# Regrouping the zero stores of a decode-attention backward kernel: four stores per step, counted over batch and kv-head together

## The chip, the core and the metric

The kernel runs on one NeuronCore of a Trainium2 chip. The metric is device time in microseconds (us). The median of the 11 runs of the kernel before is 290.94 us (289.98 to 292.38).

## What is computed

The reference is a decode step (B = 4 rows, one token each, D = 512) with its gradients. The layer is a layernorm, attention over a cache of 4096 positions of which only the last 1024 are attended, a gated feed-forward block beside it, and the residual:

```python
W = min(4096, max(256, Sk // 4))               # 1024 of Sk = 4096
k = jnp.repeat(k_cache[:, :, Sk - W:, :], rep, axis=1)
v = jnp.repeat(v_cache[:, :, Sk - W:, :], rep, axis=1)
p = softmax(einsum(q, k) * Dh ** -0.5);  o = einsum(p, v)
return x + o.reshape(B, Sq, Hq * Dh) @ wo + (gelu(xn @ w_gate) * (xn @ w_up)) @ w_down
```

The outputs are the forward result and the gradients of x, of both caches and of all weights. The gradient of a cache has the cache's shape, (4, 8, 4096, 128) in bf16. Its last 1024 positions hold dK or dV. The first 3072 positions were never attended, so their gradient is zero, and the kernel has to write these zeros: 2 caches x 4 batch rows x 8 kv-heads = 64 regions of 3072 x 128 x 2 bytes = 768 KB each, 50.3 MB in all.

## The kernel before, in words

**Stages.** Inputs are loaded, the feed-forward block is done (to about 47 us), and then a loop over t = 0..3 treats two kv-heads (g = 0, 1) of all four batch rows at a time. An iteration t does, in the order of the program: `scores(t, 0)` (transposes of the K blocks and S = qK), `softmax(t)`, `scores(t, 1)` (the same on the V blocks, dP), `softmax_d(t)`, `odq(t, 0)` (the output o), `pre(t + 1)` (projections for the next iteration from wo and wq), `odq(t, 1)` (dq), `fin(t)`, `load_next(t)`, which issues all loads of iteration t + 2. The products for dV, dK, dwo and dwq are put as small pieces in a list `bg`, and `tick(2)` takes two of them after each K or V block. Each piece is a matmul into PSUM and a copy to a staging tile by `evac` (L94 on ACT, L96 on DVE); full staging tiles (`stg_dv`, `stg_dk`, `osb_o`, `osb_q`) are stored from POOL.

**Three issuers of DMA.** SP issues all loads (wo L235, wq L237, K and V blocks `kb`, `vb` L242) and the two small last stores. POOL issues the stores of computed gradients. ACT issues the stores of zeros (L100, called from `zeros`), from a tile `ztile` of zeros on 64 partitions, in rows of 12 KB.

**Where zeros are issued.** `zeros(n)` stores the next n regions. It walks a queue of runs, and one DMA stays within one run and has at most 4 regions (GP * 2). Before the change a run is the 8 regions of one cache and one batch row. The calls: 4 regions at the end of the feed-forward part; in `scores(t, k)` at b == 1 of each g, 4 regions, but none for g = 0, k = 0 (there 2 in t = 3); 2 after `scores(0, 0)`; 2 after `odq(t, 0)` in t = 2 and t = 3; all that is left at the end. That is 18 regions up to the end of t = 0, then 12, 14 and 16 in t = 1, 2 and 3, and 4 at the end. The calls for 2 shift the runs against the calls for 4, so that several calls for 4 reach the end of a run and become two DMAs of 2 regions: 8 DMAs of 4 regions and 16 of 2. Each store is also placed behind the last `evac` on ACT.

**Completion semaphores.** The framework gives each DMA that SP or ACT issues one of eight completion semaphores in turn, in the order of the scheduled program, counted over both engines together. A DMA waits, on the engine that issues it, until the DMA that had its semaphore before it has landed. So the DMA at place n of the list waits for place n - 8, whatever the two have to do with each other, and what stands behind it on its engine waits too. POOL's stores have eight semaphores of their own. The later part of the list in the program before (x r: regions; "S" SP, "A" ACT), with the start of each issue in the profiled execution:

```
18 A zeros x4 (t0) 58.43    19 A zeros x2 61.64    20 A zeros x4 69.73    21, 22 A zeros x2, x2 76.19, 76.84
23 S wo(2) 94.95    24 S wq(2) 98.28    25, 26 S kb(2,0), kb(2,1) 103.83    27 A zeros x4 (t1) 107.27
28, 29 S vb(2,0), vb(2,1) 105.00, 117.73    30, 31 A zeros x2, x2 118.76, 119.41    32 A zeros x4 126.13
33 S wo(3) 144.14    34 S wq(3) 152.72    35, 36 S kb(3,0), kb(3,1) 153.31, 158.11
37 A zeros x2 (t2) 162.82    38, 39 S vb(3,0), vb(3,1) 158.52, 183.7
40 A zeros x2 163.47    41 A zeros x4 172.10    42, 43 A zeros x2, x2 186.27, 197.20    44 A zeros x2 200.18
45 A zeros x2 (t3) 219.17    46, 47 A zeros x2, x2 225.33, 225.98    48 A zeros x4 236.94
49, 50 A zeros x2, x2 243.76, 244.41    51 A zeros x2 246.84    52 A zeros x4 (end) 271.40
53 S out_0 273.96    54 S out_1 277.44
```

wo(t), wq(t), kb(t,g) and vb(t,g) are the loads of iteration t. Places 0 to 17 are the inputs of the feed-forward part, the loads of t = 0 and t = 1, and, at place 11, the first store of 4 regions of zeros.

Of the kernel before, what the change touches and what calls it, by code (L numbers as in the profile page):

```python
# [18 lines left out]
def kernel(  # L19
# [26 lines left out]
    nc = tc.nc  # L46

    B, Sq, D = A_x.shape
    _, G, Sk, Dh = A_k_cache.shape
# [4 lines left out]
    K0 = Sk - W  # L54
# [4 lines left out]
    GP = 2  # L59
    NT = G // GP  # L60
# [37 lines left out]
    def store(eng, out, in_, kind, apart):  # L98

        d = eng.dma_start(out=out, in_=in_)  # L100
        for k in apart:
            tc.declare_no_dep(d.ins, group=k, reason="stores write disjoint parts of the outputs")
        tc.add_to_no_dep_group(kind, d.ins)
        return d
# [54 lines left out]
    ZP = P // 2  # L159
# [92 lines left out]
                    load_kv(t + 2, k, g)  # L252


    zruns = deque([og, b, 0] for b in range(B) for og in (out_2, out_3))

    def zeros(n):


        zs = ztile[0:P:P // ZP, :]  # L260
        while n > 0 and zruns:
            og, b, g = zruns[0]
            w = min(n, G - g, GP * 2)
            zsrc = bass.AP(tensor=zs.tensor, offset=zs.offset, ap=[list(zs.ap[0]), [0, w], [1, ZW]])
            z = store(nc.scalar, og[b, g:g + w, 0:K0, :].rearrange("g (m j) d -> m g (j d)", m=ZP), zsrc, "zeros",
                      ["rest", "zeros"])
            tc.add_manual_dep(z.ins, last[-1].ins.name,
                              mybir.DependencyInfo(mybir.DependencyClass.NoSync, mybir.DependencyReason.DATA))
            n -= w
            zruns[0][2] += w  # L270
            if zruns[0][2] == G:
                zruns.popleft()


# [2 lines left out]
    def tick(n):  # L277
        for _ in range(min(n, len(bg))):
            bg.popleft()()
# [62 lines left out]
    def scores(t, k):  # L342

        lf = (qm, dom)[k][:].rearrange("p s c -> p (s c)")
        blks = (k_t, v_t)[k]
        ps = ps_a.tile([P, WQ], FP32, name="S_ps", tag=("S", "dP")[k])
        for g in range(GP):
            for b in range(B):
                T_ps = ps_w.tile([P, J, P], BF16, name="T_ps", tag="w")
                for j in range(J):  # L350
                    nc.tensor.transpose(T_ps[:, j, :], blks[(t, g)][:, b, j, :], ident[:])  # L351
                T_sb = tsb.tile([P, J * P], BF16, name="T_sb", tag="T", bufs=4)
                evac(T_sb[:], T_ps[:].rearrange("p j m -> p (j m)"), 1024, half=True)
                s = b * GP + g
                for q in range(NQ):
                    nc.tensor.matmul(ps[q * RG:(q + 1) * RG, :], lhsT=lf[:, s * RG:(s + 1) * RG],  # L356
                                     rhs=T_sb[:, q * WQ:(q + 1) * WQ], start=(g == 0 and b == 0),
                                     stop=(g == GP - 1 and b == B - 1), tile_position=(0, q * RG))
                tick(2)
                if b == 1:  # L360
                    zeros(4 if (g, k) != (0, 0) else 2 if t == NT - 1 else 0)
        st[t][("S", "dP")[k]] = ps[:]

    def by_quarter(src, nm):
# [293 lines left out]
    for f4 in range(NF4):  # L658
        held = {}
        n = min(4, NF - 4 * f4)  # L660
# [30 lines left out]
    with tc.tile_pool(name="stage", bufs=3, reuse_waits="tile") as stage, \  # L691
            tc.tile_pool(name="wodd", bufs=1, reuse_waits="tile") as wodd:
        wpool.append(wodd)
        kvpool.append(wodd)
        load_w(1)
        for k in range(2):
            load_kv(1, k, 1)
        for t in range(NT):
            if t == 0:
                pre(t)  # L700
            masks(t)
            scores(t, 0)
            zeros(2 if t == 0 else 0)
            softmax(t)
            dvdk(t, 0)
            scores(t, 1)
            softmax_d(t)
            dvdk(t, 1)
            odq(t, 0)
            zeros(2 if t >= NT - 2 else 0)  # L710
            if t + 1 < NT:
                pre(t + 1)
            odq(t, 1)
            fin(t)
            load_next(t)
            dw(t)
        tick(len(bg))
        zeros(2 * B * G)


        acc_r = kvp.tile([P, 2, ND, B, RB], FP32, name="acc_r", tag="kb")
        nc.vector.tensor_copy(out=acc_r[:], in_=acc[:].unsqueeze(4).broadcast_to([P, 2, ND, B, RB]))
        fin_ps = []
        for o in range(2):
            f_ps = ps_w.tile([P, ND, P], FP32, name="f_ps", tag="w")
            for c in range(ND):
                nc.tensor.transpose(f_ps[:, c, :], acc_r[:, o, c].rearrange("p b r -> p (b r)"), ident_f[:])
            fin_ps.append(f_ps[:])
        acc_o, acc_d = fin_ps[0].rearrange("p c d -> p (c d)"), fin_ps[1].rearrange("p c d -> p d c")

        def adj(x):
            return x[:].rearrange("p (d c) -> p d c", c=ND)

        out_b = kvp.tile([P, D], BF16, name="out_b", tag="vb")
        nc.vector.tensor_tensor(out=out_b[:], in0=acc_o, in1=x_b[:], op=ALU.add)
        nc.sync.dma_start(out=out_0.rearrange("b s d -> (b s) d"), in_=out_b[0:P:RB, :])

        s1 = const.tile([P, 1], FP32, name="s1")
        nc.vector.reduce_sum(out=s1[:], in_=acc_d, axis=AX.XY)
        pr = kvp.tile([P, D], FP32, name="pr", tag="vb")  # L740
        s2 = const.tile([P, 1], FP32, name="s2")
        nc.vector.tensor_tensor_reduce(out=adj(pr), in0=acc_d, in1=adj(xn_f), scale=1.0, scalar=0.0,
                                       op0=ALU.mult, op1=ALU.add, accum_out=s2[:])
        nm1 = const.tile([P, 1], FP32, name="nm1")
        nc.vector.tensor_scalar(out=nm1[:], in0=s1[:], scalar1=-1.0 / D, scalar2=None, op0=ALU.mult)
        nm2 = const.tile([P, 1], FP32, name="nm2")
        nc.vector.tensor_scalar(out=nm2[:], in0=s2[:], scalar1=-1.0 / D, scalar2=None, op0=ALU.mult)
        nc.vector.scalar_tensor_tensor(out=adj(pr), in0=adj(xn_f), scalar=nm2[:, 0:1], in1=acc_d,
                                       op0=ALU.mult, op1=ALU.add)
        nc.vector.tensor_scalar(out=pr[:], in0=pr[:], scalar1=nm1[:, 0:1], scalar2=rstd[:, 0:1],  # L750
                                op0=ALU.add, op1=ALU.mult)
        dx_b = kvp.tile([P, D], BF16, name="dx_b", tag="kb")
        nc.vector.tensor_tensor(out=dx_b[:], in0=pr[:], in1=dy_b[:], op=ALU.add)
        nc.sync.dma_start(out=out_1.rearrange("b s d -> (b s) d"), in_=dx_b[0:P:RB, :])
# [30 lines left out]
```

## Time and profile before

| | before |
|---|---|
| median of 11 runs | 290.94 us |
| the profiled execution, its own time | 290.05 us |
| its span, first to last instruction | 288.3 us |
| bytes moved by DMA | 112.39 MB, 390 GB/s over the span |
| PE, DVE, ACT, POOL busy | 203.3, 149.6, 116.5, 64.6 us |
| zero stores | 24 issues on ACT, 9.6 to 23.6 us from issue to landing |

In the profile, PE is the matrix engine, PEld its weight loads, DVE, ACT and POOL the vector, scalar and GpSimd engines, SP the engine that only issues DMAs. An entry such as ACTq or SPq is the issue of a DMA on that engine; a long one has stood there for a wait or for room in the queue. A bracket `[17.48 <-DMA kb...]` behind a timeline line is the idle time of the engine before that line and what released it. In the tables by stage the columns are: stretch and its length, busy time of PE, PEld, DVE, ACT and POOL with the number of instructions, granted clock of PE, share of the DMA engines (a little over 1 is possible, since packets overlap), GB/s.

### The profile page before, as it was taken

How to read it: one execution, taken by the hardware profiler on the slowest of the kernel's cores; microseconds unless marked ns; L12 is line 12 of the kernel's file. 1: busy time of each engine (PE TensorE's matmuls, PEld its weight loads, DVE VectorE, ACT ScalarE, POOL GpSimd, SP SyncE). 2: the span in 40 equal slices, each digit the busy share in tenths (PEclk: the TensorE clock that was granted, in tenths of full speed). 3: DMA queues.
4: the chain of work that ended last, by engine and by line, in shares of the span. 5: the costliest groups of instructions: out<-in, count | busy, mean ns of one | idle time of the engine just before them, and what ended most of it. 6: DMA issues, size and time to landing. Idle time of an engine off the chain costs nothing. (4 is left out here: it accounts for less than half of the span.)

```text
span 288.3 us, 7133 instructions
## 1 busy us (share of the span) xinstructions
PE 203.3 (71%) x3102; PEld 142.0 (49%) x3116; DVE 149.6 (52%) x319; ACT 116.5 (40%) x225; POOL 64.6 (22%) x82
## 2 busy tenths in 40 slices
PE   1397998758868895986989678402988678697700
PEld 0386886425546653654666355201565355463400
DVE  6374574544655664464556535400476526547840
ACT  3001665454524473543336444003455445247600
POOL 6000121613033312213321132201062132302400
PEclk9995899997979998697959969855799979869975
DMA  4999999999999999999999999999967999999994
GB/s 130 397 418 383 384 399 408 423 385 428 419 425 421 423 410 421 424 427 420 421 407 390 412 427 425 422 413 398 419 255 287 385 413 415 407 412 365 355 412 205
DMA packets 25831, 112.39 MB, mean 390 GB/s; under 512 B 1537, under 2 KB 3593, under 8 KB 20937
## 3 DMA queue, kind: packets, MB, share of 16 engines
q10 hardware_dynamic: 4612, 50.46, 41.7%
q1 hardware_dynamic: 13380, 30.81, 28.3%
q0 software_dynamic: 7808, 30.67, 26.8%
q8 instruction: 24, 0.39, 0.5%
q14 instruction: 7, 0.05, 0.0%
HBM read 30.93 MB, written 81.01 MB: 388 GB/s over the span
## 5 line engine op out<-in xcount | busy, mean ns | idle before, releaser
L96 DVE COPY T_sb<-T_ps 128x1024 bf16<-128x1024 bf16 x64 | 44.2, 691 | 30.9 <-PE T_ps L351 30.5
L94 ACT CAST stg_dv<-kv_ps 128x512 bf16<-128x512 f32 x52 | 28.3, 590 | 52.5 <-PE kv_ps L474 26.7
L94 ACT CAST stg_dk<-kv_ps 128x512 bf16<-128x512 f32 x46 | 24.9, 589 | 20.8 <-PE wqT_ps L537 8.3
L351 PE MATMUL T_ps<-ident,vb 128*128 128x128 bf16 x256 | 25.6, 245 | 0.5 <-DVE osb_q L96 0.3
L351 PE MATMUL T_ps<-ident,kb 128*128 128x128 bf16 x256 | 23.3, 220 | 0.9 <-ACT osb_g L94 0.3
L351 PEld LDWEIGHTS <-kb 128*128 128x128 bf16 x256 | 17.2, 97 | 11.2 <-issue 3.7
L351 PEld LDWEIGHTS <-vb 128*128 128x128 bf16 x256 | 19.4, 111 | 6.6 <-issue 2.5
L474 PE MATMUL kv_ps<-domr,P_q 128*128 128x512 bf16 x60 | 21.7, 420 | 0.4 <-issue 0.4
L474 PE MATMUL kv_ps<-qmr,dS_q 128*128 128x512 bf16 x59 | 19.2, 400 | 2.2 <-ACT stg_dk L94 1.2
L94 ACT CAST osb_g<-dwg_ps 128x384 bf16<-128x384 f32 (+1 forms) x30 | 14.6, 534 | 11.7 <-PE dwg_ps L650 5.7
L94 ACT CAST osb_q<-dwq_ps 128x512 bf16<-128x512 f32 x25 | 13.7, 588 | 11.8 <-PE dwq_ps L507 11.6
L96 DVE COPY woT<-woT_ps 128x1024 bf16<-128x1024 bf16 x16 | 11.1, 692 | 13.4 <-PE woT_ps L294 13.4
L94 ACT CAST osb_o<-dwo_ps 128x512 bf16<-128x512 f32 x23 | 12.6, 590 | 10.4 <-PE dwo_ps L493 6.4
L100 POOL DMA_DIRECT2D out_dram<-stg_dv x8 | 6.2, 775 | 41.9 <-ACT stg_dv L94 32.4
L367 POOL TENSOR_TENSOR dS_q<-dS_b,qmsk 128x1024 bf16<-128x1024 bf16 x4 | 7.5, 1884 | 33.0 <-DVE dS_b L420 33.0
L96 DVE COPY wqT<-wqT_ps 128x1024 bf16<-128x1024 bf16 x16 | 11.0, 689 | 6.2 <-PE wqT_ps L537 5.9
L376 PE MATMUL pT_ps<-ident,dS_b 128*128 128x128 bf16 x8 | 1.2, 242 | 18.1 <-ACT stg_dv L94 14.4
L356 PE MATMUL S_ps<-T_sb,dom 128*32 128x256 bf16 x128 | 10.0, 297 | 5.6 <-DVE T_sb L96 5.5
L537 PEld LDWEIGHTS <-wq_sb 128*128 128x128 bf16 x128 | 10.6, 116 | 6.0 <-issue 4.4
L294 PE MATMUL woT_ps<-ident,wo_sb 128*128 128x128 bf16 x128 | 13.5, 255 | 0.0
L100 POOL DMA_DIRECT2D out_dram<-stg_dk x8 | 6.1, 768 | 32.7 <-ACT stg_dk L94 13.7
L537 PE MATMUL wqT_ps<-ident,wq_sb 128*128 128x128 bf16 x128 | 12.6, 253 | 1.1 <-issue 1.1
(195 smaller groups left out, 389.2 us busy)
## 6 DMA issues: line engine op xcount, KB each, us to landing
out_dram<-ztile ACTq DMA_DIRECT2D x8, 3072.0 KB, 18.4
out_dram<-ztile ACTq DMA_DIRECT2D x16, 1536.0 KB, 13.6
kb<-in_A_k_cache_dram SPq DMA_DIRECT2D x8, 1024.0 KB, 42.0
vb<-in_A_v_cache_dram SPq DMA_DIRECT2D x8, 1024.0 KB, 34.9
out_dram<-stg_dv POOLq DMA_DIRECT2D x8, 1024.0 KB, 14.7
out_dram<-stg_dk POOLq DMA_DIRECT2D x8, 1024.0 KB, 9.5
wo_sb<-in_A_wo_dram SPq DMA_DIRECT2D x4, 1024.0 KB, 12.7
wq_sb<-in_A_wq_dram SPq DMA_DIRECT2D x4, 1024.0 KB, 29.5
```

The lines of the kernel that those rows point to most:

```text
L94: last.append(nc.scalar.copy(out=out, in_=in_))
L96: return nc.vector.tensor_copy(out=out, in_=in_)
L100: d = eng.dma_start(out=out, in_=in_)
L294: nc.tensor.transpose(wT_ps[:, i, c, :], wo_sb[:, 2 * h2 + i, c * P:(c + 1) * P], ident[:])
L351: nc.tensor.transpose(T_ps[:, j, :], blks[(t, g)][:, b, j, :], ident[:])
L356: nc.tensor.matmul(ps[q * RG:(q + 1) * RG, :], lhsT=lf[:, s * RG:(s + 1) * RG], rhs=T_sb[:, q * WQ:(q + 1) * WQ], start=(g == 0 and b == 0 ...
L367: nc.gpsimd.tensor_tensor(out=dst[:], in0=src[:].unsqueeze(1).broadcast_to([P, NQ, WQ]), in1=qmsk[:].unsqueeze(2).broadcast_to([P, NQ, WQ] ...
L376: nc.tensor.transpose(pT_ps[:, jj, :], src[:, jj * P:(jj + 1) * P], ident[:])
L474: nc.tensor.matmul(mps[:].rearrange("p b d -> p (b d)"), lhsT=src[:, q, jj * P:(jj + 1) * P], rhs=mr[:, g].rearrange("p b d -> p (b d)"), ...
L537: nc.tensor.transpose(wT_ps[:, i, c, :], wq_sb[:, c, h * Dh:(h + 1) * Dh], ident[:])
```

## The change

A run of zeros becomes all 32 regions of one cache: the batch row and the kv-head are merged into one index of B * G = 32, first all of dK's (out_2), then all of dV's (out_3). The calls change in two places: in `scores` the 2 regions of t = 3 at g = 0, k = 0 go, and after `odq(t, 0)` the 2 regions are issued in t = 1, 2 and 3 instead of t = 2 and 3. That makes 18 regions to the end of t = 0, then 14 in each of t = 1, 2 and 3 (4, 4, 4 and 2), and 4 at the end. 32 = 4 + 14 + 14, so no store meets the end of a run before it is full: 14 DMAs of 4 regions and 4 of 2.

```diff
-    zruns = deque([og, b, 0] for b in range(B) for og in (out_2, out_3))
+    zruns = deque([og, 0] for og in (out_2, out_3))
...
-            og, b, g = zruns[0]
-            w = min(n, G - g, GP * 2)
+            og, r = zruns[0]
+            w = min(n, B * G - r, GP * 2)
...
-            z = store(nc.scalar, og[b, g:g + w, 0:K0, :].rearrange("g (m j) d -> m g (j d)", m=ZP), zsrc, "zeros",
-                      ["rest", "zeros"])
+            zdst = og.rearrange("b g s d -> (b g) s d")[r:r + w, 0:K0, :].rearrange("r (m j) d -> m r (j d)", m=ZP)
+            z = store(nc.scalar, zdst, zsrc, "zeros", ["rest", "zeros"])
...
-            zruns[0][2] += w
-            if zruns[0][2] == G:
+            zruns[0][1] += w
+            if zruns[0][1] == B * G:
                 zruns.popleft()
...
                 if b == 1:
-                    zeros(4 if (g, k) != (0, 0) else 2 if t == NT - 1 else 0)
+                    zeros(4 if (g, k) != (0, 0) else 0)
...
             odq(t, 0)
-            zeros(2 if t >= NT - 2 else 0)
+            zeros(2 if t > 0 else 0)
             if t + 1 < NT:
                 pre(t + 1)
```

## The prediction

> **What bounds the kernel now.** I read the page first. 112.39 MB in 288.3 us, with the row of DMA shares at 9 almost everywhere: the kernel is bound by its transfers, and the only time to be won is time in which they run below their level. The row of GB/s shows where.
>
> ```profile
> span 288.3 us, 7133 instructions
> DMA  4999999999999999999999999999967999999994
> GB/s 130 397 418 383 384 399 408 423 385 428 419 425 421 423 410 421 424 427 420 421 407 390 412 427 425 422 413 398 419 255 287 385 413 415 407 412 365 355 412 205
> ```
>
> Then the table by stage (last column GB/s):
>
> ```profile
> 8.00:208.00 200.00, 149.91 (x2399) 106.81 (x2411) 100.96 (x215) 79.23 (x156) 42.16 (x41) 0.85 1.02 413
> 208.00:220.00 12.00, 11.27 (x206) 8.36 (x206) 8.16 (x19) 7.20 (x15) 5.28 (x4) 1.00 0.61 237
> 220.00:228.00 8.00, 6.45 (x71) 3.83 (x69) 4.66 (x8) 3.34 (x7) 1.30 (x2) 1.00 0.99 390
> 228.00:260.00 32.00, 24.39 (x353) 17.23 (x354) 16.24 (x35) 14.33 (x29) 6.56 (x6) 0.84 1.01 412
> 260.00:272.00 12.00, 9.46 (x65) 4.53 (x64) 10.05 (x17) 9.55 (x18) 4.09 (x6) 1.00 0.94 357
> ```
>
> The level is 413 GB/s. Against it 208 to 220 loses (413 - 237)/413 x 12 = 5.1 us, 220 to 228 loses 0.4, 260 to 272 loses (413 - 357)/413 x 12 = 1.6: together 7.1 us. What the first 8 us and the last 4 lose (start-up and the last landings) the change does not touch. In 208 to 220 PE is 94% busy: the compute runs flat out, but late, and has too few stores to hand over.
>
> Why is it late? The timeline just before, and the list of who waited for whom:
>
> ```profile
> 184.00:188.00 4.00, 0.10 (x1) 0.12 (x2) 1.00 (x3) 0.00 (x0) 1.88 (x1) 0.64 1.02 425
> 188.00:192.00 4.00, 0.00 (x0) 0.00 (x0) 0.00 (x0) 0.00 (x0) 0.00 (x0) 0.50 1.05 431
> 192.00:196.00 4.00, 0.00 (x0) 0.00 (x0) 0.00 (x0) 0.00 (x0) 0.00 (x0) 0.50 0.98 398
> ...
> 186.27 11.54 ACTq L100 DMA_DIRECT2D out_dram<-ztile  x2
> 197.85 2.05 ACT L94 CAST stg_dv<-kv_ps 128x512 bf16<-128x512 f32 x4 [17.48 <-DMA kb<-in_A_k_cache_dram]
> 200.18 0.61 ACTq L100 DMA_DIRECT2D out_dram<-ztile  x1
> ...
> PE pT_ps L376 <- ACT stg_dv L94: 14.4, 1, 14.4
> kb<-in_A_k_cache_dram SPq DMA_DIRECT2D x1, 1024.0 KB, 43.9
> ```
>
> ACT copies until 180.37, then does nothing for 17.48 us, and every other engine runs dry behind it. What it waits for is no data of its own: it is the issue of a zero store. Place 42 of the list waits for place 34, wq(3), which was issued at 152.72 and took 33.5 us: 186.2, and the store goes at 186.27. Place 43 waits for place 35, kb(3,0): 153.31 + 43.9 = 197.2, the release on the line above. Place 44 waits for kb(3,1), 158.11 + 42.0 = 200.1, and goes at 200.18. So the dry stretch comes from which loads stand eight places ahead of t = 2's last zero stores; the DMA engines are full in it (425, 431, 398), but afterwards the loads are through, and the stores that ACT should have prepared are not there.
>
> **The change, part by part.** *Fewer issues.* 24 zero stores become 18; same 64 regions, same 12 KB rows, so the bytes stay. On ACT an issue stands for 0.61 us (median; 2.14 at most): 6 x 0.61 = 3.7 us off ACT, 12.8 by the longest. ACT is busy 40%; I cost this at nothing, covered by the DMA engines being the bound (up to -1 us if ACT paced the last stretch).
>
> *The places shift.* I count the list anew:
>
> ```
> 22 wo(2)  23 wq(2)  24 kb(2,0)  25 kb(2,1)  26 zeros x4 (t1)  27 vb(2,0)  28 vb(2,1)  29, 30 zeros x4, x4  31 zeros x2 (new)
> 32 wo(3)  33 wq(3)  34 kb(3,0)  35 kb(3,1)  36 zeros x4 (t2)  37 vb(3,0)  38 vb(3,1)  39, 40 zeros x4, x4  41 zeros x2
> 42, 43, 44 zeros x4 each (t3)  45 zeros x2  46 zeros x4 (end)  47 out_0  48 out_1
> ```
>
> Now the store that stood at 186.27 (place 40) waits for place 32, wo(3). No view gives that landing. wo(3) is issued at 144.14, ahead of wq(3) on the same queue; wo(2) took 12.7 us, so it lands between 156.8 and 186.2. I take "before 180.4" (nearest row: wo(2)), a wait of 0; the other end is 5.9 us. Place 41 waits for wq(3), 186.2 as before. Nothing in t = 2 waits for kb(3,0) or kb(3,1) any more. The other new pairs are harmless: 29, 30, 31 and 39 wait for places 21 to 23 and 31, issued 30 us or more earlier; 36 waits for vb(2,1), as place 37 did; in t = 3 places 42 and 43 wait for kb(3,0) and kb(3,1), which `scores(3, 0)` needs before them anyway; 44 to 48 wait for things long landed. On SP, places 22 to 25 wait for older DMAs than before (one wait of 5.0 us for a V load ahead of kb(2,0) goes); its queue is backed up there, so I count 0.
>
> *The moved 2 regions.* 2 x 0.786 MB / 413 GB/s = 3.8 us of transfer go from 219 to about 130.7, right behind the second `o_x` on ACT (130.24 + 0.49). There the engines are full, so everything in flight in t = 1 and t = 2 may land up to 3.8 us later: vb(2,1), for which ACT stands before 162.82, and wq(3). Bounds 0 and 3.8; I keep both.
>
> *Sum.* ACT reaches place 40 at 180.4 to 184.2, adds four copies (2.05), `o_x` (0.51) and two issues (1.2), and place 41 is released at 186.2 to 190.0, against 200.18 for its counterpart. The compute behind it is ahead by 10 to 14 us. The stores that came at 210.50, 217.27 and 222.80 (dv, dk, dk, 1.05 MB or 2.5 us each) come by about 200, 207 and 213, and the 3.8 us of early zeros stand in the queue besides: 7.6 + 3.8 us of work against a hole of 5.1 + 0.4 us. So the hole closes. In 260 to 272 the compute is then ahead too, but ACT waits there for a staging tile (1.23 us before 264.51), which follows the DMA: I count half of 1.6. Gain 5.1 + 0.4 + 0.8 = 6.3 us. What is late next is the transfers themselves, without a hole: 112.39 MB at 413 GB/s.
>
> The profiled execution took 290.05 us, its span and 1.75 around it; it lies 0.89 below the median. 290.05 - 6.3 = 283.8; beside the median, 290.94 - 6.3 = **284.6 us**.
>
> *Unknown: the order of destinations.* All of dK's zeros come before dV's, and a store may straddle two batch rows. No row shows this. The stage means run from 398 (8 to 44 us) to 421 GB/s (160 to 180); from 44 us on (some 240 us) that is +9 to -4.6 us. I take 0, since each 12 KB row is written as before.
>
> The Trainium skill has two rules that would change the sum. "DMA: Bandwidth & Descriptors", Specifications, gives an HBM limit of about 358 GB/s per core; by it 112.39 MB need 314 us, no hole could be filled, and the change would bring nothing; the span of 288.3 us at 390 GB/s contradicts it for this core. The same page, Anatomy of one DMA, fits about 2.0 us of fixed cost to each DMA (for those issued from GpSimd); six fewer would save 12 us if they ran one after another; with the share at 1.02 the stores lie beside other transfers, and the sum would be 0 for that part.
>
> **Rivals.** *(1) The wait only changes hands.* If the schedule puts one DMA elsewhere, the last store of t = 2 falls on kb(3,0) again and goes at 197.2 to 201, as late as before. For: the list is made by a scheduler, and ACT's places drift between SP's. Against: the new store of t = 1 belongs at 130.7, wo(3) at 144.14, 13 us apart; and a drift of t = 2's first store among the V loads leaves places 39 to 41 alone. Time: 290 (289.5 to 291).
>
> *(2) Slower: the loads of t = 3 are starved.* From 163 on ACT queues 14 regions without a break (before: 10, then a pause), and dv stores join early; SP's loads share the engines. Price: the longest V load of the profile took 53.1 us; with that and 3.8, vb(3,1), issued at 183.7, lands at 240.6 instead of being there in time. It decides from 240.2, where its first transposes ran before (fifth block of `scores(3, 1)` in the chain): every us beyond is lost, with the 3.8 us of zeros that t = 3 no longer has to fill it. Against: vb(3,1)'s bytes are no more than before, and while loads are late the engines are busy with stores due anyway. Time: 293 (292 to 296).
>
> *(3) More than the holes.* Transfers at 421 GB/s and all 7.1 us won: 280. For: the stage before the stall ran at 421. Against: 412 in 228 to 260 with stores alone.
>
> That the change doesn't do what it says would show at once: 14 issues of 3072 KB and 4 of 1536 KB, and on ACT's queue 6 x 16 = 96 fewer packets than 4612.
>
> **How the numbers follow.** Forecast 0.76 (282 to 288), rival 1 0.08, rival 2 0.10, rival 3 0.06. A measurement of this kernel can tell 0.3%, 0.9 us, from no change. Faster: 0.76 + 0.06 + a quarter of rival 1 = 0.84; within: 0.06; slower: 0.10. The range 281.0 to 289.5 leaves out most of rivals 1 to 3, about 0.2; it holds the -4.6 end of the rate nearly, and a wait of 5.9 at place 40.
>
> **What would show it.** Right: ACT's idle stretch before 197.85 gone, no wait of ACT for kb; place 41 released near 186 to 190 by wq(3); 208 to 220 at 400 GB/s or more; `scores(3, 0)` starting near 205 to 210 instead of 217; compute done some 10 us before the end of the transfers, with ACT or PE waiting for staging tiles in t = 3. Wrong: a zero store that stands on ACT for another load; GB/s under 350 for 8 us anywhere between 180 and 270; PE waiting for kb or vb in t = 3 for more than 10 us.

## The result, and the profile after

The kernel after takes 288.21 us (median of 12 runs, 286.37 to 288.76) against 290.56 us of the kernel before (47 runs): ratio **0.991, 95% interval 0.9887 to 0.9932**. It is faster by 2 to 3.3 us. The forecast was 284.6 us, a gain of 6.3: the direction and the range (281.0 to 289.5) held, and a little over a third of the gain came. The ratios of the experiments below leave out runs more than 1.5% above the fastest of the same kernel, which the granted clock does not set apart; in the kernel with two regions left in t = 3 these are seven of 12 (295.1 to 297.3 us).

The page of the profiled execution (287.76 us; lines as shown of before):

```profile
span 286.1 us, 7126 instructions
DMA  5999999999999999999999999999996989999795
GB/s 135 401 414 385 385 406 428 419 423 426 420 424 422 415 415 419 424 423 419 429 417 409 402 403 423 420 427 417 422 412 251 414 368 397 423 397 374 282 408 218
```

The dip of before (255, 287 at 209 to 223 us) is now one slice (251, at 215 to 222 us), and behind it there are 368, 374 and 282, where before there were 413, 365 and 355. The table by stage, last column GB/s, in the stretches shown of before:

```profile
8.00:208.00 200.00, 157.44 (x2566) 110.92 (x2578) 107.18 (x232) 84.34 (x166) 47.40 (x45) 0.88 1.02 416
208.00:220.00 12.00, 6.93 (x57) 4.24 (x58) 3.31 (x5) 3.81 (x7) 0.32 (x1) 0.66 0.88 351
220.00:228.00 8.00, 5.64 (x61) 3.24 (x58) 5.04 (x10) 3.67 (x7) 1.55 (x3) 1.00 0.92 366
228.00:260.00 32.00, 26.31 (x379) 17.95 (x382) 16.76 (x34) 14.96 (x30) 6.76 (x6) 0.84 0.98 394
260.00:272.00 12.00, 7.83 (x36) 3.89 (x35) 8.07 (x12) 7.08 (x13) 4.07 (x6) 0.86 0.84 321
```

Against 413 GB/s the four stretches from 208 to 272 lose 1.8, 0.9, 1.5 and 2.7 us: 6.9 together, and before 7.2 (5.1, 0.4, 0.1 and 1.6). So the lost transfer time was hardly won; most of it moved. And in 208 to 220 PE, 94% busy before, is busy for 6.93 us of 12.

What ACT does, from its timeline (a bracket is its idle time before the line, and what released it):

```profile
182.24 0.61 ACTq L100 DMA_DIRECT2D out_dram<-ztile  x1
...
191.30 0.63 ACTq L100 DMA_DIRECT2D out_dram<-ztile  x1
192.03 1.56 ACT L94 CAST stg_dv<-kv_ps 128x512 bf16<-128x512 f32 x3 [4.60 <-DMA wq_sb<-in_A_wq_dram]
```

That part went as forecast: place 40 goes without a wait at 182.24, place 41 is released by wq(3) at 191.30, and 17.48 us of standing have become 4.60. But PE, from its timeline:

```profile
203.84 0.81 PE L180 MATMUL acc_ps<-od_T,wqT 128*128 128x4 bf16 x26 [0.16 <-DVE wqT L96]
211.84 1.03 PE L351 MATMUL T_ps<-ident,kb 128*128 128x128 bf16 x8 [7.20 <-DMA kb<-in_A_k_cache_dram]
...
219.72 0.62 PE L351 MATMUL T_ps<-ident,kb 128*128 128x128 bf16 x8 [1.23 <-DMA kb<-in_A_k_cache_dram]
```

In the kernel before, the same place:

```profile
216.18 0.81 PE L180 MATMUL acc_ps<-od_T,wqT 128*128 128x4 bf16 x26 [0.16 <-DVE wqT L96]
216.85 0.61 PE L351 MATMUL T_ps<-ident,kb 128*128 128x128 bf16 x8
```

The work of t = 2 is done at 204.65, some 12 us earlier than before, as the prediction said. Then PE has no K blocks: kb(3,0) was issued at 156.18 and landed at 211.8, kb(3,1) at 163.24 and 219.7. Before, they were issued at 153.31 and 158.11 and landed at 197.2 and 200.1, and `scores(3, 0)` found them there. The page's rows of DMA issues say the same (last number: median us from issue to landing; before 42.0 and 34.9):

```profile
kb<-in_A_k_cache_dram SPq DMA_DIRECT2D x8, 1024.0 KB, 55.6
vb<-in_A_v_cache_dram SPq DMA_DIRECT2D x8, 1024.0 KB, 44.8
```

**Why the loads came late** is in the table of DMA queues for a stretch. Columns: packets, MB, share of the 16 engines. q10 holds the zeros, q0 POOL's stores, q1 the loads. First the kernel after, 172 to 208 us; then the kernel before, 188 to 200 us, when ACT stood.

```profile
q10 hardware_dynamic: 871, 10.09, 66.1%
q0 software_dynamic: 883, 3.26, 22.3%
q1 hardware_dynamic: 869, 1.73, 12.5%
```

```profile
q1 hardware_dynamic: 1329, 2.63, 59.3%
q10 hardware_dynamic: 186, 1.89, 37.3%
q0 software_dynamic: 90, 0.29, 6.0%
```

In the kernel after the three queues have moved nearly the same number of packets: as long as all three hold work they take turns. (The kernel before shows the same in 172 to 180 us, where all three hold work: 212, 211 and 210 packets.) But 871 packets of zeros are 10.09 MB (11.6 KB each) and 869 packets of loads 1.73 MB (2 KB each). So the loads get 1.73 MB in 36 us, 48 GB/s of 421. In the kernel before they got 2.63 MB in 12 us, 219 GB/s, because ACT stood and its queue ran dry. The wait that the change took away had been clearing the way for the loads that the next iteration needed. (The Trainium skill, "DMA: Bandwidth & Descriptors", Queues, rings and completion order, says that a DMA engine goes round the queues that have work, one packet at a time. The equal counts agree; that a packet is 9 to 17 descriptors there, these tables can't show.)

The share of a queue is an average, and a load is there only when the last of its 16 parts is. Of kb(3,0), 15 parts had landed by 195.4 us, against 193.4 before, and the last alone came at 211.8, against 197.2. Of kb(3,1), 15 had landed by 212.3, against 197.7. So kb(3,1) is late as a whole and kb(3,0) by one part; what held up that part, no run here shows.

### The profile page after: what moved, and what is told of

Same layout as the page of the kernel before. It is cut to its first block, busy times and chain, and to the rows that moved or that the text cites. A ratio compares the mean times of both kernels' runs of the same rounds, so it can differ in the third digit from the quotient of the medians.

```text
span 286.1 us, 7126 instructions
## 1 busy us (share of the span) xinstructions
PE 205.4 (72%) x3101; PEld 140.9 (49%) x3116; DVE 149.3 (52%) x319; ACT 116.7 (41%) x225; POOL 64.6 (23%) x82
## 4 chain that ended last, share of the span: by engine, by line
PE 45%; DMA 27%; DVE 14%; issue 3%; ACT 3%; another core or an unknown queue 3%; SPq 0%; ACTq 0%; DVEq 0%
DMA out_dram<-stg_dv 18%; PE T_ps L351 12%; PE S_ps L356 5%; DMA out_dram<-osb_g 5%; PE kv_ps L474 5%; DVE T_sb L96 5%; DMA wd_sb<-in_B_w_down_dram 4%; PE dwq_ps L507 3%; PE wgT_ps L677 3%; PE dwo_ps L493 3%; PE woT_ps L294 2%; PE wdT_ps L565 2%; PE od_ps L431 1%; PE dwg_ps L650 1%
## 5 line engine op out<-in xcount | busy, mean ns | idle before, releaser
L351 PE MATMUL T_ps<-ident,kb 128*128 128x128 bf16 x256 | 26.6, 238 | 9.4 <-DMA kb<-in_A_k_cache_dram 8.4
L351 PEld LDWEIGHTS <-kb 128*128 128x128 bf16 x256 | 19.6, 107 | 27.8 <-issue 13.0
L474 PE MATMUL kv_ps<-qmr,dS_q 128*128 128x512 bf16 x59 | 20.5, 419 | 7.9 <-ACT stg_dk L94 7.1
L94 ACT CAST osb_g<-dwg_ps 128x384 bf16<-128x384 f32 (+1 forms) x30 | 14.6, 534 | 13.5 <-PE dwg_ps L650 5.5
L96 DVE COPY woT<-woT_ps 128x1024 bf16<-128x1024 bf16 x16 | 11.1, 691 | 14.5 <-PE woT_ps L294 14.5
L94 ACT CAST osb_o<-dwo_ps 128x512 bf16<-128x512 f32 x23 | 12.7, 589 | 8.8 <-PE dwo_ps L493 8.8
L96 DVE CAST stg_dk<-kv_ps 128x512 bf16<-128x512 f32 x18 | 12.1, 685 | 7.8 <-PE kv_ps L474 5.2
L294 PE MATMUL woT_ps<-ident,wo_sb 128*128 128x128 bf16 x128 | 12.7, 250 | 0.5 <-DVE stg_dv L96 0.3
L507 PE MATMUL dwq_ps<-od_r,xnm 128*128 128x256 bf16 x64 | 12.7, 326 | 0.4 <-ACT osb_o L94 0.2
L96 DVE COPY wgT<-wgT_ps 128x1024 bf16<-128x1024 bf16 x14 | 9.7, 692 | 5.3 <-PE wgT_ps L677 5.2
## 6 DMA issues: line engine op xcount, KB each, us to landing
kb<-in_A_k_cache_dram SPq DMA_DIRECT2D x8, 1024.0 KB, 55.6
wq_sb<-in_A_wq_dram SPq DMA_DIRECT2D x4, 1024.0 KB, 19.5
```

What stands on the lines that cost most here:

```text
L94: last.append(nc.scalar.copy(out=out, in_=in_))
L96: return nc.vector.tensor_copy(out=out, in_=in_)
L294: nc.tensor.transpose(wT_ps[:, i, c, :], wo_sb[:, 2 * h2 + i, c * P:(c + 1) * P], ident[:])
L474: nc.tensor.matmul(mps[:].rearrange("p b d -> p (b d)"), lhsT=src[:, q, jj * P:(jj + 1) * P], rhs=mr[:, g].rearrange("p b d -> p (b d)"), ...
L507: nc.tensor.matmul(mps[:, i].rearrange("p g d -> p (g d)"), lhsT=xnm[:, i2 * 2 + i, c:D:ND], rhs=dq_r[:].rearrange("p g d -> p (g d)"), st ...
```

## The experiments

Ratios are to the kernel before, with 95% intervals; the kernel after has 0.991. The theory at the outset: the waits of t = 2's zero stores were the stall, and zeros beside the loads of t = 3 gave most of the gain back. Rivals: the number of stores, or the order of the destinations, made the gain.

**Merged runs, the old calls.**

```diff
-                    zeros(4 if (g, k) != (0, 0) else 0)
+                    zeros(4 if (g, k) != (0, 0) else 2 if t == NT - 1 else 0)
-            zeros(2 if t > 0 else 0)
+            zeros(2 if t >= NT - 2 else 0)
```

> Merged runs, but the calls of the kernel before (2 regions at g = 0, k = 0 of t = 3 and none after odq of t = 1): 15 stores of 4 regions... counted from the calls, 20 stores in all. In t = 2 the places fall so that the store in scores(2, 1) waits for wq(3) and the 2 regions after odq wait for kb(3,0), one wait for a K load instead of two. Theory (the wait of ACT in t = 2 is what changed; the time that it freed was partly given back because the loads of t = 3 then share the engines with the zeros): ACT stands again for kb(3,0), until some 200 us; time between the two kernels, ratio to before 0.993 to 1.000. Rival A (fewer, wider stores are what gains): as after, 0.991. Rival B (the 2 regions moved from t = 3 to t = 1 are what gains): as before, 1.000.

Measured: 0.9934 [0.9904, 0.9963]. There are 19 zero stores (13 and 6), which the expectation counts wrongly. The last store of t = 2 waits for kb(3,0), and ACT stands 16.49 us until 202.44. But it stands from 185.95 and not from 180.37 as before, with more of t = 2 done, and `scores(3, 0)` starts at 214.5 instead of 216.9. By the middle value some three quarters of the gain are there, with one wait for a K load in place: not clearly apart from the kernel after, so this alone decides nothing.

**The new calls, runs of 8 as before.** The loop of `zeros` is that of the kernel before (`w = min(n, G - g, GP * 2)`), the calls those after.

> Runs of 8 regions as before, but the calls of the kernel after: 22 stores. In t = 2 the places fall on the same loads as after: the stores of scores(2, 1) and odq wait for wo(3), wq(3) or kb(3,0) only as far as the one split store reaches. By the list: the store at k = 1, g = 1 is 2 + 2, the first waits for wo(3), ... the second for wq(3), and the 2 regions after odq for kb(3,0). Theory: ACT stands for kb(3,0) at the third of them, so only part of the gain, ratio 0.993 to 1.000. Rival A (store count): 22 of 24 to 18, a third of the gain, 0.997. Rival B (moved regions): the whole gain, 0.991.

Measured: 0.9915 [0.9883, 0.9946]. The expectation misread the list: with 22 stores the last two of t = 2 wait for wo(3) and wq(3), exactly as after. Read rightly, the theory says "equal to after", and it is: `scores(3, 0)` starts at 211.9 (after: 211.8). Four stores more and the old order of destinations make no difference that shows, so neither rival holds. That the 2 moved regions make the gain by themselves (the expectation's Rival B) fits this number as well; the next kernel, which moves them too, decides.

**The waits put back.** The kernel after, with t = 2's two stores of 4 at g = 1 split in 2 and 2, so that its last stores wait for wq(3), kb(3,0) and kb(3,1) again:

```diff
-    def zeros(n):
+    def zeros(n, most=GP * 2):
-            w = min(n, B * G - r, GP * 2)
+            w = min(n, B * G - r, most)
-                    zeros(4 if (g, k) != (0, 0) else 0)
+                    zeros(4 if (g, k) != (0, 0) else 0, 2 if t == 2 and g == 1 else 4)
```

> After, with the two 4-region stores at g = 1 of t = 2 split into 2 + 2: same regions at the same places in the program, two more DMAs. The places shift so that the last three stores of t = 2 wait for wq(3), kb(3,0) and kb(3,1), as in the kernel before. Theory: ACT's idle stretch of 10 us or more for kb is back, kb(3,0) lands near 200 again because ACT issues no zeros meanwhile, and the time is that of before: ratio 0.997 to 1.003. Rivals A (20 stores instead of 24) and B (regions moved): the gain stays, 0.990 to 0.994.

Measured: 293.04 us, 1.0084 [1.0051, 1.0117], above the expected 0.997 to 1.003. The list of waits of this kernel (us in total, times, longest):

```profile
ACT stg_dv L94 <- DMA out_dram<-ztile: 14.2, 1, 14.2
...
PE pT_ps L376 <- ACT stg_dv L94: 11.1, 1, 11.1
```

The view names a zero store as what ended ACT's wait; by the list it is kb(3,0), eight places ahead. The last of the three stores goes at 205.31, when kb(3,1) lands (165.46 + 39.8; 219.7 in the kernel after). The same work with the old waits is 4.8 us slower than the kernel after. That is what taking them away is worth with the 2 regions moved, and it rules out that the moved regions make the gain. But then the rest of the change (2 regions moved up) costs 2.4 us against the kernel before, which suggested that leaving those 2 where they were would win more:

**Two regions stay in t = 3.** The kernel after, with 2 regions of dK issued in `scores(3, 0)` at g = 0 as before, and none after `odq(1, 0)`; t = 2's last stores still wait for wo(3) and wq(3).

> After, but the 2 moved regions stay where they were before (t = 3, g = 0, k = 0, as a 2-region store of the last two regions of out_2) instead of following odq of t = 1. Every other store is as after, and the places of t = 2 still fall on wo(3) and wq(3), so ACT does not stand for a K load. Theory in two parts (the wait removed wins some 4.8 us, which is the distance of the split run to after; the 2 regions moved forward cost some 2.4 us, the distance of the split run to before): ratio to before 0.980 to 0.987, better than after, kb(3,0) landing 2 to 4 us earlier than 211.8. Rival B (the moved regions are what gains): ratio 0.997 to 1.003. Rival C (the wait removed is all, the place of 2 regions does not matter): as after, 0.990 to 0.992.

Measured: 0.9958 [0.9914, 1.0002]; its runs scatter from 288.1 to 297.3, and the middle of all 12 is 295.1. So the two effects do not add; the idea falls. In its trace (a run of 291.3 us) ACT stands 9.83 us for wq(3), PE waits 3.77 us for kb until 209.10 and then 6.83 us for vb(3,1) until 240.96. In the kernel after vb(3,1) lands at 225.3. The 2 regions, put into t = 3's start, move beside the V loads.

| t = 2's last waits | 2 regions in t = 3 | moved to t = 1 |
|---|---|---|
| for wq(3), kb(3,0), kb(3,1) | 1 (before) | 1.0084 |
| for wo(3), wq(3) | 0.9958 | 0.991 (after) |

**Four and six regions of t = 2 held to the end.** If zeros crowd the loads, fewer zeros in t = 2 must bring the loads in earlier:

```diff
-                    zeros(4 if (g, k) != (0, 0) else 0)
+                    zeros(0 if (g, k) == (0, 0) or (t, g, k) == (2, 1, 1) else 4)
```

and for six, `zeros(2 if t in (1, 3) else 0)` after `odq(t, 0)` besides.

> After, with the 4 regions at k = 1, g = 1 of t = 2 not stored there but at the end (8 there). Theory of crowding: with 3.1 MB (7.6 us) less ahead of them, kb(3,0) lands near 204 instead of 211.8 and PE's 7.2 us wait before scores(3, 0) goes below 2 us; the time falls by a further 1 to 4 us, ratio to before 0.977 to 0.988. Rival (the K loads are late for a reason other than zeros, their own queue or the stores of dV): kb(3,0) still lands after 209 and PE still waits 5 us or more; ratio 0.991 or worse, as 8 regions are left for the end.

> After, with all 6 regions that t = 2 stores in scores(2, 1) at g = 1 and after odq held back to the end (10 there): no zero store of t = 2 stands behind any load of t = 3, and ACT's queue runs empty about 193. Turn-taking (the queues take turns packet by packet, so a queue of 12 KB rows leaves the 2 KB rows of the loads 46 GB/s while it lasts): from about 193 on the loads run at 200 GB/s or more, kb(3,0) lands by 200, kb(3,1) by 204, PE does not wait for either; but the zeros run out in 208 to 220, so a hole of 3 us or more opens there. Time within 1 us of holding four (ratio to before 0.985 to 0.994): what the loads win the hole gives back. Rival (with the loads early the whole chain moves up and the end with it): ratio 0.980 or less.

Measured: 0.9896 [0.9852, 0.994] and 0.9902 [0.9864, 0.9941]. kb(3,0) lands at 206.2 and 198.0 instead of 211.8, and with six PE no longer waits for it. But the table by stage of the kernel with six held shows that nothing takes the place of the held zeros (last column GB/s):

```profile
193.00:208.00 15.00, 14.03 (x310) 9.99 (x308) 9.21 (x20) 6.82 (x14) 4.87 (x4) 0.94 0.94 363
208.00:220.00 12.00, 10.05 (x107) 5.84 (x104) 8.24 (x15) 7.18 (x14) 2.31 (x4) 1.00 0.74 286
```

1.8 and 3.7 us are lost there, and the held zeros lengthen the end: from PE's last work to the last landing it is 23.2 us instead of 13.6. What the loads win the hole gives back.

**Zeros in 6 KB rows, on 128 partitions.** If turns go by packets, halving the row halves the zeros' share without changing their number of bytes:

```diff
-    ZP = P // 2
+    ZP = P
```

> After, with the zeros stored from 128 partitions in rows of 6 KB instead of 64 partitions and 12 KB: same stores, same waits, same bytes. Crowding as a matter of row size (the queues take turns row by row, so wide rows take the larger share): the loads of t = 3 get more, kb(3,0) lands 4 us or more before 211.8, zero stores take longer to land than 16.6 us (median), ratio to before 0.980 to 0.989. Crowding as a matter of bytes in the queue alone: kb(3,0) lands at 211 +- 2, ratio as after, 0.990 to 0.993.

Measured: 0.991 [0.987, 0.995]. The queues of this kernel, 180 to 200 us, and one of its waits:

```profile
q10 hardware_dynamic: 863, 5.12, 61.4%
q1 hardware_dynamic: 864, 1.72, 22.3%
```

```profile
ACT osb_o L94 <- DMA vb<-in_A_v_cache_dram: 12.3, 1, 12.3
```

Equal packets again, but the loads now move 1.72 MB in 20 us, 86 GB/s, and kb(3,0) and kb(3,1) land at 190.1 and 203.0, over 16 us earlier than after. Two things are mixed in this. In t = 2 the first zero store now stands 12.3 us for vb(2,1), until 171.1 (place 36 waits for place 28), and with few zeros in the queues the loads move 1.47 MB in 172 to 180 us, against 0.38 in the kernel after. The row size by itself shows in the first kernel of "An earlier start with all zeros stored", which has the narrow rows without this wait. The time stays, since PE, which no longer waits for kb, starts `scores(3, 0)` at 210.1, held up by ACT's wait (without it, in that later kernel, the work of t = 2 is done at 203.8).

**Narrow rows with four staging tiles, and with regions held.** Four `stage` buffers instead of three, paid for with three `T_sb` instead of four; then the same with four and with six regions of t = 2 held.

> As the 6 KB rows, with four staging tiles for dV and dK instead of three (the smaller zero tile and three T_sb tiles instead of four make room). Theory of what is late next (in t = 3 the copies of dK stand for the store of the first dV tile, 10.6 us of ACT waits in after, and the queues run dry meanwhile, 207 GB/s in 264 to 268): those waits go below 3 us, 260 to 272 is back at 380 GB/s or more, and the time is 2 to 4 us below the 6 KB rows alone. Rival (the store of the dV tile only marks the transfers' own level): waits of the staging tiles go, but the time stays within 1 us of the 6 KB rows alone.

> A version that should beat both kernels: 4 regions of t = 2 held to the end, rows of 6 KB, four staging tiles. If the K loads of t = 3, the share of the loads and the staging tiles are three separate losses, their gains add: ratio 0.975 to 0.984. Rival (all three act on the same stretch, and the end is set by the transfers' own total and by the lagging engines at the end): no better than the 6 KB rows with four staging tiles, 0.985 to 0.991.

> As the one before with 6 regions held. Separate losses: 0.973 to 0.984. Same stretch: 0.985 to 0.992, with a hole in 208 to 220 as in the 12 KB version with six held.

Measured: 0.9887 [0.9843, 0.993], 0.9937 [0.9912, 0.9963] and 0.9987 [0.9946, 1.0028]. Four staging tiles alone are not clearly apart from three (0.991). Narrow rows and held regions, which each free the loads, do not add up: with both, 208 to 220 runs at 202 and 238 GB/s for want of stores, and ACT still stands 13 to 14 us for vb(2,1).

**The held regions put into the hole.** Six are held as above, but four of them go behind `fin(2)`, when the K loads are through; in a second kernel 2 more go behind `odq(2, 1)` (the line above `fin(t)` in the diff is the second kernel's alone):

```diff
-            zeros(2 if t > 0 else 0)
+            zeros(2 if t in (1, 3) else 0)
...
             odq(t, 1)
+            zeros(2 if t == 2 else 0)
             fin(t)
+            zeros(4 if t == 2 else 0)
```

> The kernel after, but of t = 2 the last store of 4 regions goes from scores(2, 1) to behind fin(2), and the 2 regions behind odq(2, 0) go to the end (6 there). Theory (the loads of t = 3 are late only while ACT's zero queue is full beside them; what is lost otherwise is lost in stretches without stores): the 4 regions fall into the stretch 208 to 220 us, which in the kernel with six regions held back to the end ran at 286 GB/s (3.7 us lost of 12). kb(3,0) and kb(3,1) land by about 198 to 205 as there, 208 to 220 runs at 380 GB/s or more, and the ratio to before is 0.980 to 0.988. Rival (what the zeros win in one stretch they take from the loads or from the last stretch, so that the lost time only moves): the ratio stays at 0.990 (0.987 to 0.993), with the loss found at another place, such as 240 to 272, or behind vb(3, 0) and vb(3, 1).

> As the kernel with 4 regions behind fin(2), but 2 regions more go behind odq(2, 1), and 4 instead of 6 are left for the end. Theory: 193 to 208 us, which ran at 363 GB/s with six regions held back (1.8 us lost of 15), is filled too, by 1.6 MB or 3.8 us of zeros; ratio 0.977 to 0.988, and not above the one without these 2. Rival (crowding): the 2 regions stand beside vb(3, 0) and vb(3, 1), which land 4 us or more later than without them, and the ratio is no better than there (0.988 to 0.993).

Measured: 0.9895 [0.986, 0.9929] and 0.9947 [0.9914, 0.9981]. In the first the hole is closed as expected: 208 to 220 runs at 410 GB/s, and `scores(3, 0)` starts at 204.9. The rival wins all the same. PE's timeline in the first kernel:

```profile
234.09 1.03 PE L351 MATMUL T_ps<-ident,vb 128*128 128x128 bf16 x8 [5.55 <-DMA vb<-in_A_v_cache_dram]
```

The four regions of 203.7 now crowd vb(3,1), which lands at 234.0, 44.6 us after its issue, and the hole is in 252 to 264 (291 GB/s). In the second it lands at 237.5, and 228 to 240 runs at 216 GB/s.

**Zeros left out.** By then every version filled one hole and got another. Is the kernel bound by its bytes at all? Three kernels leave out the zeros of t = 2, of t = 3, or of t = 1 to 3.

```diff
-                    zeros(4 if (g, k) != (0, 0) else 0)
+                    zeros(4 if (g, k) != (0, 0) and t != 2 else 0)
-            zeros(2 if t > 0 else 0)
+            zeros(2 if t in (1, 3) else 0)
-        zeros(2 * B * G)
+        zeros(4)
```

(and likewise for t = 3 and for t = 1 to 3.)

> The kernel after without the 14 regions of zeros of t = 2 (11.0 MB, 26.7 us of transfer at 413 GB/s are left out; 28 + 18 + 4 regions are stored). Theory (the loads of t = 3 were late because they took turns with t = 2's zeros): kb(3,0) and kb(3,1) land before 195 us (211.8 and 219.7 in the kernel after), scores(3, 0) starts by 200, and everything behind it is as much earlier: the time is 268 to 274 us. Rival (scores(3, 0) could not have started before about 205 to 210 for the work of t = 2 in front of it, loads or not): it starts there, and the time is 278 to 286.

> The kernel after without the 14 regions of zeros of t = 3 (11.0 MB, 26.7 us of transfer left out); t = 2's zeros stay and delay the loads of t = 3 as they did, so scores(3, 0) starts at 209 to 213 us. Theory (behind that start the work of t = 3 sets the end as much as the bytes do): the time falls by less than half of 26.7, to 275 to 285 us, with the DMA engines half empty between 220 and 270. Rival (the bytes alone set the end, and the holes are only what the stores at hand do not fill): 262 to 270 us.

> The kernel after without the zeros of t = 1, 2 and 3 (42 of 64 regions, 33 MB, 80 us of transfer at 413 GB/s are left out). By bytes alone the time would be near 208 us; what it is instead is the work's own length. Theory (the computation has little slack of its own, so that in the whole kernel it is late as soon as its loads are): 240 to 260 us. Rival (the computation has much slack, and only bytes and waits count): below 235 us.

Measured: 274.74, 284.3 and 266.35 us (two runs each; before on that chip 290.12). Against the 288.2 us of the kernel after, the first wins 13 of 26.7 us of transfer left out, the second only 4 (as its theory had it), and the third 22 of 80: its 266 us are above even the theory's 240 to 260, so the work has less slack than the theory gave it. The row of GB/s of the kernel without t = 3's zeros, its last quarter nearly empty, beside a time of 284.3 us:

```profile
GB/s 148 407 413 385 385 396 405 423 407 432 418 421 425 420 406 424 414 424 420 427 420 410 420 397 432 417 429 418 424 410 290 236 75 150 150 2 183 368 414 217
```

(The two runs of this kernel are 286.02 and 282.57 us.) So the bytes alone do not set the end: behind a late start of t = 3 its work does. In the kernel without t = 2's zeros the loads are quick,

```profile
kb<-in_A_k_cache_dram SPq DMA_DIRECT2D x8, 1024.0 KB, 24.6
```

kb(3,0) and kb(3,1) land at 179.5 and 183.3, and `scores(3, 0)` starts at 203.0 without any wait. That is between the expectation (by 200) and its rival (205 to 210): 7.2 us of the 211.8 were PE's wait for kb(3,0), and about 203 is where the work of t = 2 ends with the zeros of t = 1 in place (196.4 without those too).

From the traces, per kernel, in us of the span: the first transpose of kb in t = 3, the end of PE's last instruction, the end of the span, and the two differences.

| kernel | scores(3, 0) starts | PE ends | span | start to PE's end | rest |
|---|---|---|---|---|---|
| before | 216.9 | 273.6 | 288.3 | 56.8 | 14.7 |
| after | 211.8 | 272.5 | 286.1 | 60.7 | 13.6 |
| waits put back | 220.1 | 275.6 | 290.1 | 55.5 | 14.5 |
| six held | 207.2 | 264.3 | 287.5 | 57.0 | 23.2 |
| four behind fin(2) | 204.9 | 268.2 | 284.9 | 63.4 | 16.7 |
| t = 2's zeros left out | 203.0 | 259.8 | 273.3 | 56.7 | 13.6 |
| t = 3's zeros left out | 213.0 | 269.9 | 284.3 | 56.9 | 14.4 |
| t = 1 to 3's left out | 196.4 | 249.2 | 263.6 | 52.8 | 14.4 |

From the start of `scores(3, 0)` on there are about 57 us of work (52.8 without the zeros of t = 1 to 3, and over 60 where loads or stores hold it up) and 14 us from PE's last work to the last landing: 71 us. By these rows the kernel has two ends of nearly equal length, this one and the bytes, and whoever moves one finds the other.

**An earlier start with all zeros stored.** The narrow rows brought the K loads in by 203 but had ACT stand for vb(2,1). One more place in t = 1 takes that wait away (the store of t = 2 then waits for a zero store):

```diff
-    ZP = P // 2
+    ZP = P
...
-                    zeros(4 if (g, k) != (0, 0) else 0)
+                    for n in ((2, 2) if (t, g, k) == (1, 1, 1) else (0,) if (g, k) == (0, 0) else (4,)):
+                        zeros(n)
```

> The kernel with 6 KB rows of zeros, and in t = 1 the store of 4 regions in scores(1, 1) at g = 1 split into 2 and 2, so that the first store of t = 2 waits for a zero store and not for vb(2,1), which held ACT for 12.3 us there; t = 2's last two still wait for wo(3) and wq(3). Theory (two ends of about equal length: the start of scores(3, 0) plus some 71 us of work, and the bytes, about 281 us of span): kb(3,0) and kb(3,1) land by 203 us, scores(3, 0) starts at 203 to 207 (210.1 with the wait), the work would end at 274 to 278, and the bytes set the end: 283 to 286 us, ratio 0.974 to 0.985. Rival (what is won at the start of scores(3, 0) goes into waits for staging tiles and loads later, as in all versions so far): 287 to 289 us, ratio 0.988 to 0.994.

> As the kernel with 6 KB rows and the split store in t = 1, with the 2 regions behind odq(2, 0) held to the end (6 there), so that t = 2's last store waits for wo(3). Theory: scores(3, 0) starts 0 to 4 us earlier than without holding, and the 2 regions at the end are 3.8 us of transfer; the time is that of the kernel without holding within 1.5 us, since there the bytes set the end. Rival (the work sets the end there too): 2 us or more below it.

> As the kernel with 6 KB rows and the split store in t = 1, with four staging tiles (and three instead of four T_sb), so that ACT's copies of t = 3 wait less for stores to land. If the work behind scores(3, 0) is stretched by these waits, 1 to 2.5 us below the kernel with three staging tiles, and t = 3 from its first scores to the last work of PE takes 57 us or less; if the bytes set the end, the same within 1 us.

Measured: 0.9877 [0.9841, 0.9913], 0.9921 [0.9892, 0.995] and 0.9865 [0.983, 0.9899] (286.07 us, the lowest median of all). The first (286.39 us) falls between its two expectations: 0.4 us above the theory's 283 to 286 and, by its ratio, just below the rival's 0.988 to 0.994. The second (288.0), with the 2 regions behind `odq(2, 0)` held, is 1.6 us above it, just outside the theory's 1.5 and against the rival; none of the three is clearly apart from the kernel after. PE's timeline in the first:

```profile
206.54 0.62 PE L351 MATMUL T_ps<-ident,kb 128*128 128x128 bf16 x8 [2.75 <-DMA kb<-in_A_k_cache_dram]
...
220.41 1.03 PE L351 MATMUL T_ps<-ident,kb 128*128 128x128 bf16 x8 [7.67 <-DMA kb<-in_A_k_cache_dram]
```

Without ACT's wait at 160 its queue is full again, and kb(3,1), which had landed at 203.0, lands at 220.4; 8 us of that are its later issue (169.57 instead of 161.70, by one place more in the list). The queues of this kernel in 172 to 208 us, to be set beside those of the kernel after:

```profile
q10 hardware_dynamic: 1339, 7.96, 53.1%
q0 software_dynamic: 1165, 4.33, 29.6%
q1 hardware_dynamic: 1334, 2.68, 19.2%
```

Zeros and loads take equal turns again, and with 6 KB rows the loads get 2.68 MB, 74 GB/s, where beside 12 KB rows they got 1.73. That shows the turn-taking by its size, with no wait of ACT mixed in. The K loads gain little by it: kb(3,0) takes 51.5 us from issue to landing instead of 55.6. So most of what the landings at 190.1 and 203.0 had won came with ACT's wait. It is the change of this study in small: take away a wait of ACT, and the loads behind it pay. With four staging tiles `scores(3, 0)` starts at 211.2 and t = 3 up to PE's end takes 60.0 us, not 57 or less; the time is that of three tiles within 1 us, as expected if the tiles are not what sets the end.

## Why the prediction was right and wrong, point by point

**The list, right.** 14 stores of 4 and 4 of 2, and the places 22 to 48 as counted. The guess for wo(3), "before 180.4", held: place 40 goes at 182.24 without a wait. Rival 1 (the wait falls on kb(3,0) again) did not occur.

**ACT's stall, right.** Place 41 was forecast for 186.2 to 190.0 and went at 191.30. The dv and the first dk store came at 198.2 and 204.9 (forecast 200 and 207). With the waits put back by split stores the kernel is 4.8 us slower. "Fewer issues" at nothing was right too: 22 stores instead of 18, with the same waits, take the same time.

**The step that failed** is "everything in flight in t = 1 and t = 2 may land up to 3.8 us later", and with it "So the hole closes". The price was taken from the bytes of the 2 moved regions, and asked only of vb(2,1) and wq(3); wq(3) landed 5.1 us later. What counts is that ACT, no longer standing, keeps its queue full from about 168 to 208 us; in 172 to 208 the zeros take 66.1% of the engines. kb(3,0) landed 14.6 us later than before and kb(3,1) 19.5, against a bound of 3.8; 2.9 and 5.1 us of this are their later issue. `scores(3, 0)` started at 211.84, not 205 to 210, and the third of the three stores came at 219.7, not 213. The held regions and the left-out zeros moved these landings the way this account says; the 6 KB rows moved the loads' share that way, and the landings by little on their own. That the time stayed inside the range is in part luck: what the prediction names for a late end of it, a wait of 5.9 us at place 40, did not come.

**The premise was half the truth.** "The kernel is bound by its transfers, and the only time to be won is time in which they run below their level": with t = 3's zeros left out, 26.7 us of transfer less, only 4 us are won. A hole in GB/s was the sign of late work, and not by itself the loss. The account that fits both profiled spans goes by the work: `scores(3, 0)` starts 5.0 us earlier, the stretch from there to PE's end is 3.9 us longer, the rest 1.1 shorter: 2.2 us, the difference of the spans. Of the 3.9, 1.5 are in `scores(3, 0)` itself (12.3 us instead of 10.8 from its first to its last transpose, with the wait of 1.23 for kb(3,1)). Another 1.5 come with dv's store: it takes 14.2 us from issue to landing instead of 12.7, and ACT waits for its staging tile, 2.55 us where it was 1.23 (the kernel after, then before):

```profile
262.50 2.12 ACT L94 CAST stg_dk<-kv_ps 128x512 bf16<-128x512 f32 x4 [2.55 <-DMA out_dram<-stg_dv]
264.51 2.12 ACT L94 CAST stg_dk<-kv_ps 128x512 bf16<-128x512 f32 x4 [1.23 <-DMA out_dram<-stg_dv]
```

The remaining 0.9 us have no line of their own.

**The rivals.** Rival 2 named the mechanism (the loads of t = 3 starved by an unbroken zero queue) but the wrong loads: it looked at vb(3,1), due at 240.2, which in the kernel after landed in time at 225.3. The K loads, ahead of it, paid. Its own case came in the kernel with two regions left in t = 3, where vb(3,1) landed at 240.9. It was one outcome with the forecast rather than the other side of it: 4.8 us won by the waits, and part given back. Rival 3 (421 GB/s and all holes won) did not occur. The rate in 8 to 208 is 416 GB/s against 413, which by the bytes is 1.5 of the 2.2 us; but the kernel with the new calls and runs of 8 takes the same time at 413 there, so the gain does not hang on it.

**The signs.** Of those named for "right", 208 to 220 ran at 351 GB/s and not at 400, and `scores(3, 0)` came too late. Of those named for "wrong", the only load other than wq(3) for which a zero store stood in t = 2 was vb(2,1), until 165.6, as foreseen; PE waited 8.4 us for kb in t = 3, short of the 10; but GB/s under 350 for 8 us did come, 320 in 212 to 220 and again 294 in 264 to 272.

**Open.** Why the last part of kb(3,0) lands 16 us behind the 15 others. Why the 2 moved regions cost 2.4 us where the waits are put back. Why the runs with two regions left in t = 3 scatter by 9 us. Whether an order of zeros exists that reaches the span of 281 us or so that the bytes ask for (288.3 less the 7.2 lost): of those tried none is clearly better than the kernel after.

## What to carry to other kernels

Before a wait on an issuing engine is taken away, ask what ran while it stood: the queue that it kept empty may have been the way of a load that someone needs next. Price such crowding by packets in turn (row width of each queue, for as long as all are full), not by the bytes that were added; and ask when the last part of a load lands, not only what share its queue gets. And a hole in the transfer rate is time to be won only if the work that follows is not late on its own: leave the filler out once, and the time that remains is the length of the work.

## What the hardware showed unexpectedly

- Three full queues moved 871, 883 and 869 packets in 36 us, with rows of 11.6, 3.7 and 2.0 KB; with 6 KB rows of zeros, 863 of zeros against 864 of loads. So here the share of a full queue went by the size of its rows.
- One 1 MB load is 16 parts, and they land far apart: those of kb(3,0) between 169.4 and 211.8 us in the kernel after, 15 of them by 195.4.
- An issue of zeros stands 0.38 us on ACT from 128 partitions in 6 KB rows, and 0.61 us from 64 partitions in 12 KB rows.
